# Loading v two tokens to a partition, with half-size attention tiles, wider q and k runs and a new opening order, in a fused chunk-attention and feed-forward kernel

## The chip, the cores and the metric

The kernel runs on one core of one Trainium2 chip. The metric is the device time of one execution, in microseconds (us); each kernel is run several times and the median is quoted.

Engines have these names in the profile: PE is TensorE's matmul, PEld its weight load, DVE is VectorE, ACT is ScalarE, POOL is GpSimd, SPq is the queue on which SyncE issues DMA. A matmul instruction of the program appears as one LDWEIGHTS (PEld) and one MATMUL (PE), 2,576 of each in the profile of the kernel before; the text calls the two together a *pair*.

## The reference, cut to what matters

```
q, k, v: 8 x 8 x 576 x 64 (batch, head, token, d), float32;   4608 tokens in all
for every chunk of 64 tokens of every head:
    attn = softmax(q_c @ k_c.T / 8);   out_c = attn @ v_c        # 64x64 and 64x64
x = out, heads side by side                                      # 4608 x 512
h = x @ w_in                                                     # 512 -> 2048
g = h * sigmoid(beta * h)                                        # beta: one number per hidden unit
result = g @ w_out                                               # 2048 -> 512
```

The kernel works in nine blocks of 512 tokens (eight chunks, 8 heads). For each block it computes the attention, then the two large products. `mm1` is a group of four 128x512 matmuls of the hidden layer, `mm2` one of the output layer; a block has 16 of each.

## The kernel before

The parts that the change touches. A matmul of the attention uses one quarter of TensorE's array: a 64x64 tile. (The profile writes 64*64 for it, and 128*128 for a large matmul.) The trace of this kernel shows the score pairs in fours, one for each quarter: four start 3 to 4 ns apart, then there is a step, mostly of 21 or 22 ns, to the next four, about 32 ns from group to group. `scores` puts out 16 pairs per call (half of them in the opening), `attend` 32.

```
def load_beta():                                  # 2,048 descriptors of 4 bytes
    e.dma_start(beta_raw[:, :], beta.rearrange("(t p) -> p t", p=128))
    ...                                           # beta_half = beta_raw * 0.5 on VectorE

def load_qk(blk, which, halves=(0, 1)):           # runs of 1 KB: 4 tokens x 64 x 4 bytes
    ...
    a = src[b][:, 64 * c:64 * (c + m), :].rearrange("(hp hb) (s i) d -> s hp hb (i d)", hb=2, i=4)

def load_v(blk, pairs=(0, 1, 2, 3)):              # runs of 256 bytes: one token to a partition
    ...
    e.dma_start(vstage[r:r + 64 * m, s, at // 2, h, :],
                v[b][h, 64 * c:64 * (c + m), :].rearrange("h t d -> t h d"))

def scores(blk, hp, halves=(0, 1)):
    ...
    for cc in range(2 * halves[0], 2 * halves[-1] + 2):
        for g in range(2):
            for hb in range(2):
                def f(e, cc=cc, g=g, hb=hb):
                    r, col = slice(64 * hb, 64 * hb + 64), 256 * w + 64 * cc
                    return e.matmul(A[64 * g:64 * g + 64, 2 * u + hb, col:col + 64],
                                    kT[r, 2 * cc + g, :], qT[r, 2 * cc + g, :])
...
def attend(blk, u, ps=A, psname="A", bank0=0, halves=(0, 1)):
    ...
                return e.matmul(ps[64 * half:64 * half + 64, bank, col:col + 65],
                                E[r, 2 * u + hb, 256 * w + 64 * cc:256 * w + 64 * cc + 64],
                                v_bf[r, sa, cc, 4 * u + 2 * w + hb, 0:65])
...
first = [ (load_qk, 0, 0, (1,)), (cast_qk, 0, 0, 1, "act"), ...     # hand-made order of blocks 0 to 2
```

From block 3 on a fixed plan interleaves attention with `mm1` and `mm2`; per block there are two bursts of score matmuls and two of V products, 32 pairs each, with large matmuls between them.

The softmax here doesn't subtract the row's maximum and nothing guards it: scores larger than these inputs give would overflow.

Of the kernel before, what the change touches and what calls it, by code (L numbers as in the profile page):

```python
# [166 lines left out]
def bass_chunk_attention__then__act_swish_beta_kernel(nc, q, k, v, w_in, w_out, beta, out):  # L167
# [8 lines left out]
    with ExitStack() as es:  # L176
# [7 lines left out]
        beta_raw = sb("beta_raw", [128, NT], F32)  # L184
# [6 lines left out]
        qkstage = sb("qkstage", [128, NQS, 2, 2, 4, 256], F32)  # L191
        vstage = sb("vstage", [128, NVS, 4, H, 64], F32)
        qkcast = sb("qkcast", [128, 2, 4, 4, 2, 64], BF16)
        qkT = sb("qkT", [128, 2, 4, 4, 128], BF16)
        qkO = sb("qkO", [128, 4, 2, 4, 32, 4], BF16)
        NVA = 2
        v_bf = sb("v_bf", [128, NVA, 4, H, 66], BF16)
        E = sb("E", [128, 4, 512], BF16)
        rec = sb("rec", [128, 2, 16], F32)
        x_sb = sb("x_sb", [128, 2, 2, 4, 128], BF16)  # L200
        NXT = 2
        xT = sb("xT", [128, NXT, 2, 2, 4, 128], BF16)
# [13 lines left out]
        def chunk_pairs(blk):  # L216

            if blk == REST:
                return [(b, CPB - 1, 1, b) for b in range(B)]
            return [(blk - (blk > REST), c, 2, c) for c in range(0, 8, 2)]  # L220


        def make_constants():
            P.op("pool", lambda e: e.memset(identity[:, :], 1.0), writes=[K("identity")])
            P.op("pool", lambda e: e.affine_select(
                out=identity[:, :], in_=identity[:, :], compare_op=ALU.is_equal, fill=0.0,
                base=0, pattern=[[-1, 128]], channel_multiplier=1),
                reads=[K("identity")], writes=[K("identity")])
            for sa in range(NVA):
                P.op("pool", lambda e, sa=sa: e.memset(v_bf[:, sa, :, :, 64:66], 1.0),  # L230
                     writes=[K("ones", sa)])
# [5 lines left out]

        def load_beta():
            def f(e):
                with nc.allow_non_contiguous_dma(reason="beta is tiny"):  # L240
                    return e.dma_start(beta_raw[:, :], beta.rearrange("(t p) -> p t", p=128))
            P.dma("act", f, writes=[K("beta_raw")])
            P.op("dve", lambda e: e.tensor_single_scalar(
                beta_half[:, :], beta_raw[:, :], 0.5, ALU.mult),
                reads=[K("beta_raw")], writes=[K("beta_half")])
# [4 lines left out]
        def load_qk(blk, which, halves=(0, 1)):  # L250
            s, src = blk % NQS, (q, k)[which]
            for b, c, m, at in chunk_pairs(blk):
                if at // 4 not in halves:
                    continue

                def f(e, b=b, c=c, m=m, at=at):
                    a = src[b][:, 64 * c:64 * (c + m), :].rearrange(
                        "(hp hb) (s i) d -> s hp hb (i d)", hb=2, i=4)
                    r = 64 * (at % 2)
                    return e.dma_start(qkstage[r:r + 64 * m, s, which, :, at // 2, :], a)  # L260
                P.dma("sp", f, writes=[K("qkstage", s, which, at + i, v=blk) for i in range(m)])

        def load_v(blk, pairs=(0, 1, 2, 3)):
            s, us, h = blk % NVS, (0, 1), slice(0, H)
            for b, c, m, at in chunk_pairs(blk):
                if at // 2 not in pairs:
                    continue

                def f(e, b=b, c=c, at=at, m=m):
                    r = 64 * (at % 2)  # L270
                    return e.dma_start(vstage[r:r + 64 * m, s, at // 2, h, :],  # L271
                                       v[b][h, 64 * c:64 * (c + m), :].rearrange("h t d -> t h d"))
                P.dma("sp", f, writes=[K("vstage", s, u, at + i, v=blk)
                                       for u in us for i in range(m)])
# [43 lines left out]
        def cast_qk(blk, which, half, eng):  # L318
            s, r = blk % NQS, slice(2 * half, 2 * half + 2)
            copy_cast(eng, qkcast[:, which, r, :, :, :].rearrange("p n i h d -> p h (n i) d"),  # L320
                      qkstage[:, s, which, :, r, :].rearrange("p h n (i d) -> p h (n i) d", i=4),
                      [K("qkstage", s, which, 4 * half + c, v=blk) for c in range(4)],
# [9 lines left out]
        def order_qk(blk, hp, eng):  # L332
            copy_cast(eng, qkO[:, hp, :, :, :, :].rearrange("k w n t i -> k (w n) t i"),
                      qkT[:, :, :, :, :].rearrange("k w n i (t h) -> k h (w n) t i", h=4)[:, hp],
# [3 lines left out]
        def transpose_pe(blk, which, half, ps, psname, bank, eng):  # L338
            r = slice(2 * half, 2 * half + 2)
            dst = ps[:, bank, :].bitcast(BF16).rearrange("p (i n t) -> p i n t", n=2, i=4)  # L340
            for n in range(2):
                for i in range(4):
                    P.op("pe", lambda e, n=n, i=i: e.transpose(  # L343
                        dst[:, i, n, :],
                        qkcast[:, which, 2 * half + n, i, :, :].rearrange("p h d -> p (h d)"),
                        identity[:, :]),
                        reads=[K("qkcast", which, half, v=blk), K("identity")],
                        writes=[K(psname, bank, v=("t", blk, which, half))])
            copy_cast(eng, qkO[:, :, which, r, :, :].rearrange("k h n t i -> k h (n t) i"),
                      dst.rearrange("k i n (t h) -> k h (n t) i", h=4),  # L350
# [3 lines left out]
        def cast_v(blk, eng, cc, us=(0, 1)):  # L354
            s, sa, h = blk % NVS, blk % NVA, slice(4 * us[0], 4 * us[-1] + 4)
            copy_cast(eng, v_bf[:, sa, cc, h, 0:64], vstage[:, s, cc, h, :],
                      [K("vstage", s, u, 2 * cc + g, v=blk) for u in us for g in range(2)],
                      [K("v_bf", sa, u, cc, v=blk) for u in us])



        def scores(blk, hp, halves=(0, 1)):
            u, w = divmod(hp, 2)
            qT, kT = (qkO[:, hp, which, :, :, :].rearrange("k n (c t) i -> k (n c) (t i)", c=2)
                      for which in range(2))
            for cc in range(2 * halves[0], 2 * halves[-1] + 2):
                for g in range(2):
                    for hb in range(2):
                        def f(e, cc=cc, g=g, hb=hb):
                            r, col = slice(64 * hb, 64 * hb + 64), 256 * w + 64 * cc  # L370
                            return e.matmul(A[64 * g:64 * g + 64, 2 * u + hb, col:col + 64],  # L371
                                            kT[r, 2 * cc + g, :], qT[r, 2 * cc + g, :])
                        P.op("pe", f, reads=[K("qkO", hp, which, half, v=blk)
                                             for which in range(2) for half in halves],
                             writes=[K("A", 2 * u + hb, v=("s", blk, halves))])

        def exp(blk, bank):
            P.op("act", lambda e: e.activation(E[:, bank, :], A[:, bank, :], AF.Exp, scale=0.125),  # L378
                 reads=[K("A", bank, v=("s", blk, (0, 1)))],
                 writes=[K("E", bank, half, v=blk) for half in range(2)])  # L380

        def exp_half(blk, u, half):
            dst, src = (a[:, 2 * u:2 * u + 2, :].rearrange("p b (w c) -> p b w c", w=2)[
                :, :, :, 128 * half:128 * half + 128] for a in (E, A))
            P.op("act", lambda e: e.activation(dst, src, AF.Exp, scale=0.125),  # L385
                 reads=[K("A", 2 * u + hb, v=("s", blk, (half,))) for hb in range(2)],
                 writes=[K("E", 2 * u + hb, half, v=blk) for hb in range(2)])
# [3 lines left out]


        def attend(blk, u, ps=A, psname="A", bank0=0, halves=(0, 1)):
            sa, nh = blk % NVA, len(halves)
            for cc in range(2 * halves[0], 2 * halves[-1] + 2):
                for hb in range(2):
                    for w in range(2):
                        for g in range(2):
                            def f(e, cc=cc, hb=hb, w=w, g=g):
                                r, half = slice(64 * g, 64 * g + 64), g ^ w  # L400
                                bank = bank0 + nh * g + cc // 2 - halves[0]
                                col = 65 * (2 * (cc % 2) + hb)
                                return e.matmul(  # L403
# [105 lines left out]
        def attention(blk, t0, u):  # L509
            for hp in range(4):  # L510
                at(t0 + (hp // 2) * u, scores, blk, hp)
# [216 lines left out]
```

## Time and profile before

| | before |
|---|---|
| time, median of 3 runs (range) | 301.92 us (301.12 to 302.09) |
| span of the profiled execution | 299.5 us |
| first `mm1` matmul starts | 21.54 us |
| first score burst of block 4 | 110.28 us |
| first score burst of block 8 | 228.73 us |
| last matmul starts | 295.97 us |
| block period in the steady part | 29.56 us |

First, a few lines of the profile page: busy time by engine, DMA packets, the queue that brings instructions, and the group of score matmuls (line, engine, operation, tile and shape, count, then busy us and mean ns).

```profile
PE 281.0 (94%) x2576; PEld 145.5 (49%) x2576; DVE 149.3 (50%) x244; ACT 158.7 (53%) x268; POOL 104.5 (35%) x95
...
DMA packets 106627, 55.98 MB, mean 187 GB/s; under 512 B 78952, under 2 KB 98408, under 8 KB 106600
...
q8 instruction: 20, 0.33, 0.5%
...
L371 PE MATMUL A<-qkO 64*64 64x64 bf16 x576 | 9.0, 200 | 1.1 <-ACT E L385 1.1
```

PE is busy 94% of the span, so the time can fall only by less work on PE or by fewer waits of PE.

Next, the chain of waits in a regular block (start, length, what), then the timeline of PE around one score burst.

```profile
169.47 0.37 PE A L371 x32
169.84 0.97 PE F L464 x4
...
199.02 0.38 PE A L371 x32
199.40 0.75 PE F L464 x3
```

```profile
168.44 1.03 PE L482 MATMUL F<-w_out_bf,g 128*128 128x512 bf16 x4
169.40 0.44 PE L371 MATMUL A<-qkO 64*64 64x64 bf16 x32
169.77 1.04 PE L464 MATMUL F<-xT,w_in_bf 128*128 128x512 bf16 x4
```

The chain returns to the same point after 199.40 - 169.84 = 29.56 us, and holds nothing but PE: a steady block is TensorE's own time. By the single records a burst takes 309 ns from the last large matmul to its first start, 253 ns between its first and last start, and 125 ns to the next large matmul. Of these 687 ns, 216 are the large matmul's own, so a burst costs 0.471 us.

The opening, in the timeline of PE and of the other engines (waits stand in brackets):

```profile
6.19 5.61 SPq L271 DMA_DIRECT2D vstage<-in_v_dram  x4
...
16.87 0.17 DVE L243 TENSOR_SCALAR beta_half<-beta_raw 128x16 f32<-128x16 f32 x1 [2.43 <-DMA beta_raw<-in_moe_beta_dram]
...
16.96 0.62 POOL L316 CAST v_bf<-vstage 128x512 bf16<-128x512 f32 x1 [1.51 <-DMA vstage<-in_v_dram]
```

```profile
17.63 0.44 PE L403 MATMUL F<-v_bf,E 64*64 64x65 bf16 x16 [1.06 <-POOL v_bf L316]
...
19.14 1.03 PE L444 MATMUL F<-identity,x_sb 128*128 128x128 bf16 x8 [0.86 <-DVE x_sb L426]
...
21.54 1.01 PE L464 MATMUL F<-xT,w_in_bf 128*128 128x256 bf16 x4
```

SyncE spends 5.61 us issuing four loads of v; the last v tile and beta both hold the work up to about 17 us. That is what the change is aimed at.

### The profile page before, as it was taken

How to read it: one execution, taken by the hardware profiler on the slowest of the kernel's cores; microseconds unless marked ns; L12 is line 12 of the kernel's file. 1: busy time of each engine (PE TensorE's matmuls, PEld its weight loads, DVE VectorE, ACT ScalarE, POOL GpSimd, SP SyncE). 2: the span in 40 equal slices, each digit the busy share in tenths (PEclk: the TensorE clock that was granted, in tenths of full speed). 3: DMA queues.
4: the chain of work that ended last, by engine and by line, in shares of the span. 5: the costliest groups of instructions: out<-in, count | busy, mean ns of one | idle time of the engine just before them, and what ended most of it. 6: DMA issues, size and time to landing. Idle time of an engine off the chain costs nothing.

```text
span 299.5 us, 6088 instructions
## 1 busy us (share of the span) xinstructions
PE 281.0 (94%) x2576; PEld 145.5 (49%) x2576; DVE 149.3 (50%) x244; ACT 158.7 (53%) x268; POOL 104.5 (35%) x95
## 2 busy tenths in 40 slices
PE   0669999999999999999999999999999999999995
PEld 0447855766554444444444444444444444444442
DVE  0458876766698533643364337433733373443300
ACT  3558964675676546444644464446444745544311
POOL 1135653634062594069177409540750000000000
PEclk9999999999999999999999999999999999999999
DMA  6999999999999968999947992898471122000121
GB/s 176 237 334 376 338 246 348 302 326 252 212 283 179 230 192 229 178 271 314 184 113 232 267 207 70 245 277 157 65 91 39 45 70 72 36 35 35 63 79 70
DMA packets 106627, 55.98 MB, mean 187 GB/s; under 512 B 78952, under 2 KB 98408, under 8 KB 106600
## 3 DMA queue, kind: packets, MB, share of 16 engines
q1 hardware_dynamic: 99408, 46.15, 64.9%
q10 hardware_dynamic: 7192, 9.45, 9.2%
q8 instruction: 20, 0.33, 0.5%
q14 instruction: 7, 0.06, 0.1%
HBM read 36.71 MB, written 9.44 MB: 154 GB/s over the span
## 4 chain that ended last, share of the span: by engine, by line
PE 79%; SPq 9%; DMA 8%; POOL 1%; ACT 1%; DVE 1%; issue 1%; ACTq 0%
PE F L482 39%; PE F L464 34%; SPq L260 5%; DMA wstage<-in_moe_w_out_dram 3%; DMA qkstage<-in_q_dram 2%; PE A L464 2%; DMA vstage<-in_v_dram 2%; SPq L289 2%; PE A L403 2%; SPq L271 2%; PE A L371 2%; POOL w_out_bf L305 1%; DVE qkO L316 0%; ACTq L496 0%; ACT ostage L488 0%
## 5 line engine op out<-in xcount | busy, mean ns | idle before, releaser
L482 PE MATMUL F<-w_out_bf,g 128*128 128x512 bf16 x576 | 145.0, 379 | 0.8 <-POOL w_out_bf L305 0.8
L473 DVE SCALAR_TENSOR_TENSOR g<-tt,F 128x512 bf16<-128x512 bf16 (+1 forms) x140 | 88.5, 634 | 108.1 <-ACT tt L469 107.8
L469 ACT ACTIVATE tt<-F,beta_half 128x512 bf16<-128x512 f32 (+1 forms) x140 | 89.9, 645 | 96.4 <-PE F L464 92.8
L464 PE MATMUL F<-xT,w_in_bf 128*128 128x512 bf16 (+1 forms) x560 | 130.3, 359 | 0.2
L482 PEld LDWEIGHTS F<-w_out_bf,g 128*128 128x128 bf16 x576 | 55.2, 98 | 63.3 <-POOL w_out_bf L305 0.9
L464 PEld LDWEIGHTS F<-xT,w_in_bf 128*128 128x128 bf16 x560 | 53.0, 98 | 52.2 <-DVE g L473 0.5
L316 POOL COPY qkO<-qkT 128x1024 bf16<-128x1024 bf16 x21 | 41.6, 2026 | 56.5 <-DMA qkT<-qkcast 47.3
L316 POOL CAST qkcast<-qkstage 128x1024 bf16<-128x1024 f32 x29 | 30.8, 1073 | 35.2 <-DMA qkstage<-in_k_dram 20.1
L488 ACT ACTIVATE ostage<-F 128x512 f32<-128x512 f32 x36 | 21.5, 598 | 19.7 <-PE F L482 19.7
L426 DVE TENSOR_TENSOR x_sb<-A,rec 128x1024 bf16<-128x1024 f32 (+1 forms) x19 | 20.6, 1084 | 0.7
L464 PE MATMUL A<-xT,w_in_bf 128*128 128x256 bf16 x144 | 19.9, 275 | 0.9 <-POOL w_in_bf L295 0.9
L469 ACT ACTIVATE tt<-A,beta_half 128x256 bf16<-128x256 f32 x36 | 16.4, 474 | 6.3 <-PE A L464 6.3
L316 POOL CAST v_bf<-vstage 128x512 bf16<-128x512 f32 x28 | 16.5, 625 | 6.5 <-DMA vstage<-in_v_dram 6.5
L473 DVE SCALAR_TENSOR_TENSOR g<-tt,A 128x256 bf16<-128x256 bf16 x36 | 14.7, 418 | 4.9 <-ACT tt L469 4.6
L378 ACT ACTIVATE E<-A 128x512 bf16<-128x512 f32 x28 | 16.3, 592 | 0.7 <-PE A L371 0.7
L464 PEld LDWEIGHTS A<-xT,w_in_bf 128*128 128x128 bf16 x144 | 13.9, 99 | 4.4 <-DVE g L473 1.5
L343 PE MATMUL A<-identity,qkcast 128*128 128x128 bf16 x48 | 4.5, 249 | 7.9 <-ACT qkcast L314 7.4
L305 POOL CAST w_out_bf<-wstage 128x2048 bf16<-128x2048 f32 x4 | 7.6, 1896 | 11.0 <-DMA wstage<-in_moe_w_out_dram 11.0
L371 PEld LDWEIGHTS A<-qkO 64*64 64x64 bf16 x576 | 6.6, 113 | 8.1 <-issue 4.4
L295 POOL CAST w_in_bf<-wstage 128x2048 bf16<-128x2048 f32 (+1 forms) x5 | 7.8, 1555 | 7.2 <-DMA wstage<-in_moe_w_in_dram 5.9
L371 PE MATMUL A<-qkO 64*64 64x64 bf16 x576 | 9.0, 200 | 1.1 <-ACT E L385 1.1
L403 PEld LDWEIGHTS A<-v_bf,E 64*64 64x64 bf16 x528 | 6.0, 109 | 7.0 <-issue 4.7
(36 smaller groups left out, 81.0 us busy)
## 6 DMA issues: line engine op xcount, KB each, us to landing
out_dram<-ostage ACTq DMA_DIRECT2D x36, 256.0 KB, 2.9
qkstage<-in_q_dram SPq DMA_DIRECT2D x32, 256.0 KB, 4.8
qkstage<-in_k_dram SPq DMA_DIRECT2D x32, 256.0 KB, 5.9
vstage<-in_v_dram SPq DMA_DIRECT2D x32, 256.0 KB, 6.6
wstage<-in_moe_w_out_dram SPq DMA_DIRECT2D x4, 1024.0 KB, 9.4
wstage<-in_moe_w_in_dram SPq DMA_DIRECT2D x3, 1024.0 KB, 11.9
wstage<-in_moe_w_in_dram SPq DMA_DIRECT2D x2, 512.0 KB, 9.3
qkstage<-in_q_dram SPq DMA_DIRECT2D x8, 128.0 KB, 3.7
```

Of the source, the lines that this page charges most:

```text
L260: return e.dma_start(qkstage[r:r + 64 * m, s, which, :, at // 2, :], a)
L305: P.op("pool", lambda e: e.tensor_copy(w_out_bf[:, 4 * j:4 * j + 4, :], wstage[:, j, :].rearrange("p (t d) -> p t d", t=4)), reads=[K("wst ...
L316: P.op(eng, lambda e: e.tensor_copy(dst, src), reads, writes)
L371: return e.matmul(A[64 * g:64 * g + 64, 2 * u + hb, col:col + 64], kT[r, 2 * cc + g, :], qT[r, 2 * cc + g, :])
L378: P.op("act", lambda e: e.activation(E[:, bank, :], A[:, bank, :], AF.Exp, scale=0.125), reads=[K("A", bank, v=("s", blk, (0, 1)))], write ...
L403: return e.matmul(ps[64 * half:64 * half + 64, bank, col:col + 65], E[r, 2 * u + hb, 256 * w + 64 * cc:256 * w + 64 * cc + 64], v_bf[r, sa ...
L426: P.op("dve", lambda e: e.tensor_tensor(dst, o[:, :, :, 0:64], r.unsqueeze(3).to_broadcast([128, nb, 4, 64]), ALU.mult), reads=src + [K("r ...
L464: P.op("pe", lambda e, c=c: e.matmul(ps[:, bank, r], w_in_bf[:, c, 128 * t:128 * t + 128], x_of(sx, c, halves), start=(c == 0), stop=(c == ...
L469: P.op("act", lambda e: e.activation(tt[:, T % NTT, r], ps[:, bank, r], AF.Tanh, scale=beta_half[:, t:t + 1]), reads=[K(psname, bank, v=(" ...
L473: P.op("dve", lambda e: e.scalar_tensor_tensor(g2[:, sg, t, r], tt[:, T % NTT, r], 1.0, ps[:, bank, r], ALU.add, ALU.mult), reads=[K(psnam ...
L482: P.op("pe", lambda e, t=t: e.matmul(ps[:, bank, :], g2[:, sg, t, 128 * s:128 * s + 128], w_out_bf[:, t, :], start=(t == 0), stop=(t == NT ...
L488: P.op("act", lambda e: e.activation(ostage[:, N % NOS, :], ps[:, bank, :], AF.Copy, scale=0.5), reads=[K(psname, bank, v=("o", N))], writ ...
```

## The change

The intent: v in runs of 512 bytes and q and k in runs of 2 KB (fewer, larger packets and half the issues), beta in 64 descriptors instead of 2,048, and an opening order remade for the earlier data. With two tokens of v on a partition, a chunk of 64 tokens lies on 32 partitions. So the score matmul of a chunk becomes two of 64 rows by 32 columns (even and odd keys), and its V product two of 32 rows by 64 columns that add up in PSUM. These are half the size and twice the number, so that eight instead of four cover the array.

```
-        beta_raw = sb("beta_raw", [128, NT], F32)
+        beta_raw = sb("beta_raw", [128, 32], F32)
+        beta_T = sb("beta_T", [128, 32], F32)
...                                            # load_beta
-                    return e.dma_start(beta_raw[:, :], beta.rearrange("(t p) -> p t", p=128))
+            for j in range(4):
+                P.dma("act", lambda e, j=j: e.dma_start(
+                    beta_raw[32 * j:32 * j + NT, :],
+                    beta.rearrange("(t j p) -> j t p", j=4, p=32)[j]), ...)
+        def turn_beta():                       # a 32x32 transpose on VectorE, then the half
...                                            # load_qk
-                        "(hp hb) (s i) d -> s hp hb (i d)", hb=2, i=4)
+                        "(hp hb) (s i) d -> s hp hb (i d)", hb=2, i=8)
...                                            # load_v
-                                       v[b][h, 64 * c:64 * (c + m), :].rearrange("h t d -> t h d"))
+                        a = v[b][h, 64 * c:64 * (c + m), :].rearrange("h (p i) d -> p h (i d)", i=2)
...                                            # scores
-                            return e.matmul(A[64 * g:64 * g + 64, 2 * u + hb, col:col + 64],
-                                            kT[r, 2 * cc + g, :], qT[r, 2 * cc + g, :])
+            for i in range(2):
+                for c in range(4):
+                    for hb in range(2):
+                            return e.matmul(A[32 * c:32 * c + 32, 2 * half + hb, col:col + 64],
+                                            kT[r, c, i::2], qT[r, c, :])
...                                            # attend
+                                        E[r, 2 * half + hb, at:at + 64],
+                                        v_bf[r, sa, half, 2 * hp + hb, i, 0:65],
+                                        start=(i == 0), stop=(i == 1))
...                                            # and the order of blocks 0 to 2, wholly new;
                                               # from block 3 on the same places in the plan
```

## The prediction

> **What bounds the kernel now.** TensorE, after a slow opening. The table of busy time by stretches shows it busy nearly all the time from 50 us, clock 1.00. A token block takes 29.56 us (same point of successive blocks in the chain of waits: 169.84, 199.40): 32 groups of four 128x512 matmuls at 0.864 us = 27.65, plus 1.91 for attention (four bursts of 32 matmuls, 0.48 us each, about 0.09 of it the mode change). Such spacings, summed over all matmuls, give 274 us of work in the 299.5 us span: 17 us are lost before the first hidden-layer matmul at 21.5 us, 5 between 21.5 and 80, 3.4 in the tail.
>
> **What the opening waits for** (timeline of 0 to 36 us): loads. First q lands at 4.9 us, last q/k about 11.0, last v tile about 16.9. SyncE spends 0.65 us per q/k issue and 1.4 per v issue, 11 us for block 0. In the DMA records a 256 B packet took 23 ns, 1 KB 53, 2 KB 93; the 4 B beta packets 10 ns each, 2048 of them 1.3 us over 16 engines.
>
> **What changes.**
> - DMA, block 0: q/k 6.8 us to 5.9; v 5.9 to about 4 (estimate: 512 B near 32 ns); beta 1.3 to 0. Some 4 us less before block 0 is complete, 2.8 us less per later block. SyncE issues: about 6 us instead of 11 (estimate).
> - TensorE: score and V-product matmuls double, 1152 to 2304. [...] In the trace four tiles start 3.3 ns apart and the next four follow after 32 ns, so eight starts (27 ns) should just fit into the same 32. [...] I expect 0.48 to 0.55 us per burst of 64: 0 to 2.5 us in all.
> - Exp, normalize, casts, transposes keep their sizes.
> - New order, estimated from measured durations: q/k complete near 9 us, scores of half 0 near 10.5, last V product 15.7, four normalizations on DVE (0.9 each) to 17.4, turns and copies to 18. First hidden-layer matmul at 18.0 us (17 to 19.5) instead of 21.5. w_in comes 4 us earlier, so most of this survives; stalls between there and 80 us go from 5 to 3 to 5.
>
> **Sum:** 301.9 - 3.5 (opening) - 1.3 (later stalls) + 1.0 (tiles) - 0.5 (beta, order) = 297.6 us. Range 293.8 to 301.3. Faster by over 2% (under 295.9): 0.26; within 2%: 0.68; slower: 0.06.
>
> **What would show it.** First hidden-layer matmul near 18 us; last v cast near 14; block period 29.6 to 29.9; DMA packets under 512 B down from 79k to a few thousand; TensorE gaps between 20 and 80 us no larger than before.
>
> **What would make it wrong.**
> - TensorE cannot be fed more than 32 load-and-multiply pairs in a row at 4 ns a pair: this trace has no longer burst. [...]
> - Four row tiles writing four PSUM banks, or stride-2 stationary reads, run slower.
> - The order lets the hidden layer begin even earlier (16.5), or DMA relief removes nearly all later stalls: over 2% faster.
> - ACT or DVE, 0.43 to 0.47 us per half tile against 0.44 of TensorE, become the limit once loads do not.

The term for the tiles, +1.0, stands on the trace's 3.3 ns and 32 ns alone: that eight half-size tiles would start as close together as four old ones, and so 0.48 to 0.55 us a burst, was the author's estimate. What the text calls the mode change is the passage from large to small matmuls: 309 ns from start to start there instead of 216, hence its 0.09 us.

## The result

The changed kernel takes **312.61 us** (310.55 to 313.4, four runs, correct) against 301.88 us (301.12 to 302.09) of the kernel before on the same chip. The ratio is 1.035, with a 95% interval of 1.030 to 1.040: slower. A ratio here is the mean time of one kernel's fast runs over the mean of the other's fast runs of the same rounds, so it isn't quite the ratio of the medians.

| start of | before, us | after, us | difference |
|---|---|---|---|
| first `mm1` matmul | 21.54 | 22.83 | +1.29 |
| first score burst of block 4 | 110.28 | 116.95 | +6.67 |
| first score burst of block 8 | 228.73 | 239.83 | +11.10 |
| last matmul | 295.97 | 308.06 | +12.09 |

So three losses have to be explained: an opening that should have been 3.5 us shorter and isn't, about 5.4 us between the opening and block 4, and 4.43 us over four regular blocks, which is 1.11 us a block.

The page of the changed kernel, the same lines:

```profile
PE 287.9 (92%) x3687; PEld 155.4 (50%) x3728; DVE 147.5 (47%) x250; ACT 159.2 (51%) x269; POOL 102.1 (33%) x92
...
DMA packets 76220, 56.12 MB, mean 180 GB/s; under 512 B 39320, under 2 KB 58776, under 8 KB 76184
...
q8 instruction: 29, 0.48, 0.6%
...
L376 PE MATMUL A<-qkO 64*32 64x64 bf16 x1152 | 13.0, 199 | 1.8 <-DVE qkO L322 1.1
```

The number of pairs has grown from 2,576 to 3,728 (by PEld), and the packets of instructions with it, from 20 to 29. The packets under 512 B have halved, to 39,320.

The chain of waits in a regular block, and the timeline around one score burst:

```profile
178.29 0.65 PE A L376 x64
178.94 0.97 PE F L452 x4
...
208.92 0.65 PE A L376 x64
209.57 0.97 PE F L452 x4
```

```profile
177.26 1.03 PE L470 MATMUL F<-w_out_bf,g 128*128 128x512 bf16 x4
178.22 0.72 PE L376 MATMUL A<-qkO 64*32 64x64 bf16 x64
178.87 1.04 PE L452 MATMUL F<-xT,w_in_bf 128*128 128x512 bf16 x4
```

The period is now 209.57 - 178.94 = 30.63 us, 1.07 more, and again the chain holds almost only PE. The records of the burst's 64 matmul starts have this form: the first 32 follow each other in 3 to 5 ns (one step of 16), then comes a single gap of 105 ns, and then the rest follow at 8 or 9 ns each (two steps of 34). A burst spans 537 ns for scores and 523 for V products, with 309 ns before and 118 after it. By the same reckoning it costs 0.748 us (309 + 537 + 118 - 216) or 0.734 us instead of 0.471. Two bursts of each kind a block give 2 x 0.277 + 2 x 0.263 = 1.08 us, which is the lengthening of the period.

The opening, on the DMA side first: SyncE's issue of v takes 4.70 us from 3.58 instead of 5.61 from 6.19, and the last v cast starts at 15.17 us, 1.8 us earlier. PE's timeline then shows what came of it:

```profile
3.58 4.70 SPq L278 DMA_DIRECT2D vstage<-in_v_dram  x4
...
15.17 0.42 DVE L322 CAST v_bf<-vstage 128x512 bf16<-128x512 f32 x1
```

```profile
15.31 0.44 PE L399 MATMUL F<-v_bf,E 32*64 32x65 bf16 x30
18.99 0.26 PE L399 MATMUL F<-v_bf,E 32*64 32x65 bf16 x2 [3.24 <-issue]
18.99 0.56 PE L399 MATMUL A<-v_bf,E 32*64 32x65 bf16 x32
...
22.83 1.49 PE L452 MATMUL A<-xT,w_in_bf 128*128 128x256 bf16 x6
```

```profile
42.38 0.51 PE L399 MATMUL A<-v_bf,E 32*64 32x65 bf16 x11
45.67 0.29 PE L399 MATMUL A<-v_bf,E 32*64 32x65 bf16 x21 [2.77 <-issue]
```

PE stops twice in the middle of a burst: at 15.5 us after 30 of 32 pairs, all of whose data had the same producers, and at 42.7 us after 11 of 32. "issue" means that the profile shows nothing that PE waited for, neither a tile nor a semaphore. (From start to start, counting weight loads too, these gaps are 3.48 and 2.97 us.) After the second one the clock drops, as the table by stretches shows (stretch, length, busy us of PE, PEld, DVE, ACT, POOL, then granted clock, DMA share and GB/s):

```profile
45.70:46.20 0.50, 0.50 (x24) 0.43 (x25) 0.04 (x1) 0.00 (x0) 0.03 (x1) 1.00 1.04 385
46.20:49.60 3.40, 3.18 (x44) 1.60 (x44) 1.91 (x5) 0.78 (x2) 2.52 (x2) 0.50 1.09 357
49.60:53.00 3.40, 3.35 (x84) 2.08 (x84) 2.09 (x6) 1.37 (x3) 0.89 (x2) 0.99 1.12 328
```

TensorE runs at half clock for 3.4 us. That is about 1.7 us of lost work (an estimate: half of 3.4). The drop comes at 46.22 us, 0.56 us after the end of the gap of 2.97 us. That the gap is its cause isn't shown: in run 5 below a gap of 1.87 us was, in the profiled execution of run 3 one of 2.14 us was not. The fastest of the four runs, 310.55 us, was the only one with a mean granted clock of 1.000; the other three had 0.995 and took 312.5 to 313.4 us.

The opening runs at half clock too, in both kernels, which the "1.00" of the tables hides: the trace's first clock record stands at 22.9 us (before) and 25.7 us (after). Until then `mm1` matmuls of 256 columns start 213 ns apart, afterwards 109. Eight such matmuls of the changed kernel on either side of that point (timeline of PE from 22.8 to 27 us):

```profile
22.83 1.91 PE L452 MATMUL A<-xT,w_in_bf 128*128 128x256 bf16 x8
...
26.00 1.04 PE L452 MATMUL F<-xT,w_in_bf 128*128 128x256 bf16 x8
```

So the changed kernel works on `mm1` for 2.9 us at half clock, the kernel before for 1.4; that is some 0.8 us more of lost work (an estimate: half of the difference). It also means that the start of the first `mm1` alone does not measure a lead: what comes before that point goes at half speed (213 ns instead of 109 for those matmuls).

### Where the gaps come from: the position in the program

If one counts PE's and PEld's instructions from the beginning (with the few waits of PE's own sequencer that the trace has, 5 before the first gap and 11 before the second), the gap at 15.5 us comes after the 449th and the one at 42.7 us after the 1,216th. With 64 added these are 513 and 1,280: a multiple of 256, or one past it. The 64 are fitted; what they stand for isn't shown (instructions that stand ahead of the profiled ones would give such a constant). Beside that the DMA records show one 16 KB packet on the instruction queue for about every 256 instructions: 20 packets for 5,152 in the kernel before, 29 for 7,456 in the changed one, with two instructions to each pair. The first column below is the boundary, in program order counted with those 64.

| kernel, boundary | PE reached the 256 before it at | packet ran | PE stopped | PE went on | after the packet's end |
|---|---|---|---|---|---|
| before, 512 | 15.54 us | 18.83 to 19.99 | no (reached it at 26.57) | | |
| after, 512 | 12.07 us | 16.61 to 17.72 | 15.51 | 18.98 | 1.26 us |
| after, 1280 | 38.92 us | 43.07 to 44.23 | 42.70 | 45.66 | 1.43 us |
| after, 2048 | 64.56 us | 65.73 to 66.71 | 67.23 | 68.12 | 1.42 us |

These read as one story: each packet is the next 256 instructions, and at all three stops TensorE went on only after the packet had ended, 1.26 to 1.43 us later. In the busy opening the first packet begins 3.3 us (before) and 4.5 us (after) after PE reached the 256 before it. In the kernel before, these 256 instructions last 11.0 us (15.54 to 26.57), and nothing stops. In the changed kernel bursts use them up in 3.4 us (12.07 to 15.51). (These times are counted from PE's own place. Packets can also come ahead of it: late in the changed kernel's trace, five of the last seven packets begin 0.4 to 2.0 us before PE reaches that place. So they are not the delay of a request.) In all, the changed kernel loses 7.4 us in such gaps; the kernel before, none.

So far this is a reading of one trace. The runs below test it.

### The profile page after: what moved, and what is told of

Read it like the earlier page. It is cut to its first block, busy times and chain, and to the rows that moved or that the text cites. A ratio compares the mean times of both kernels' runs of the same rounds, so it can differ in the third digit from the quotient of the medians.

```text
span 311.6 us, 8295 instructions
## 1 busy us (share of the span) xinstructions
PE 287.9 (92%) x3687; PEld 155.4 (50%) x3728; DVE 147.5 (47%) x250; ACT 159.2 (51%) x269; POOL 102.1 (33%) x92
## 2 busy tenths in 40 slices
DMA packets 76220, 56.12 MB, mean 180 GB/s; under 512 B 39320, under 2 KB 58776, under 8 KB 76184
## 4 chain that ended last, share of the span: by engine, by line
PE 84%; DVE 6%; issue 4%; DMA 3%; ACT 1%; ACTq 1%; DVEq 0%
PE F L470 38%; PE F L452 35%; DVE g L461 4%; PE A L399 3%; PE A L376 3%; PE A L452 3%; DMA beta_raw<-in_moe_beta_dram 2%; DMA qkstage<-in_q_dram 1%; DVE qkO L322 1%; PE A L433 1%; DVE x_sb L417 1%; ACT tt L457 1%; PE F L433 1%; PE A L347 0%; ACTq L484 0%
## 5 line engine op out<-in xcount | busy, mean ns | idle before, releaser
L457 ACT ACTIVATE tt<-F,beta_half 128x512 bf16<-128x512 f32 (+1 forms) x149 | 93.9, 635 | 104.0 <-PE F L452 100.4
L470 PE MATMUL F<-w_out_bf,g 128*128 128x512 bf16 x535 | 138.3, 381 | 3.3 <-issue 1.5
L452 PE MATMUL F<-xT,w_in_bf 128*128 128x512 bf16 (+1 forms) x596 | 135.4, 354 | 0.2 <-DVE g L461 0.2
L322 POOL CAST qkcast<-qkstage 128x1024 bf16<-128x1024 f32 x27 | 27.9, 1045 | 30.5 <-DMA qkstage<-in_q_dram 15.2
L384 ACT ACTIVATE E<-A 128x512 bf16<-128x512 f32 x36 | 20.6, 592 | 2.8 <-PE A L376 2.8
L452 PE MATMUL A<-xT,w_in_bf 128*128 128x256 bf16 x108 | 16.0, 286 | 0.0
L399 PEld LDWEIGHTS A<-v_bf,E 32*64 32x64 bf16 x1056 | 9.8, 105 | 11.0 <-issue 8.0
L399 PE MATMUL A<-v_bf,E 32*64 32x65 bf16 x1056 | 12.4, 204 | 2.8 <-issue 2.8
L376 PE MATMUL A<-qkO 64*32 64x64 bf16 x1152 | 13.0, 199 | 1.8 <-DVE qkO L322 1.1
L457 ACT ACTIVATE tt<-A,beta_half 128x256 bf16<-128x256 f32 x27 | 12.5, 477 | 4.2 <-PE A L452 2.9
L376 PEld LDWEIGHTS A<-qkO 64*32 64x32 bf16 x1152 | 10.7, 91 | 7.9 <-issue 5.5
```

What stands on the lines that cost most here:

```text
L322: P.op(eng, lambda e: e.tensor_copy(dst, src), reads, writes)
L376: return e.matmul(A[32 * c:32 * c + 32, 2 * half + hb, col:col + 64], kT[r, c, i::2], qT[r, c, :])
L384: P.op("act", lambda e: e.activation(E[:, bank, :], A[:, bank, :], AF.Exp, scale=0.125), reads=[K("A", bank, v=("s", blk))], writes=[K("E" ...
L399: return e.matmul(ps[64 * w:64 * w + 64, c, col:col + 65], E[r, 2 * half + hb, at:at + 64], v_bf[r, sa, half, 2 * hp + hb, i, 0:65], start ...
L452: P.op("pe", lambda e, c=c: e.matmul(ps[:, bank, r], w_in_bf[:, c, 128 * t:128 * t + 128], x_of(sx, c, halves), start=(c == 0), stop=(c == ...
L457: P.op("act", lambda e: e.activation(tt[:, T % NTT, r], ps[:, bank, r], AF.Tanh, scale=beta_half[:, t:t + 1]), reads=[K(psname, bank, v=(" ...
```

## The experiments

The theory, called F, is *feeding*: TensorE loses time because more instructions have to be brought to it, on two scales. In a burst, the pairs after the first 32 come slower (8 to 9 ns each after a gap of 105 ns, instead of 3 to 5 ns); and in the opening program packets land too late for bursts (the gaps of 3.48 and 2.97 us). The rivals are T, that half-size *tiles* are slow as such (four row tiles that write four PSUM banks, strided weights), and O, that the new opening *order* waits more by itself.

### 1. The changed kernel with v by one token again

The change but for its first part: v and tiles as before (1,152 attention matmuls, bursts of 32), with the q, k and beta loads and the opening order of the changed kernel. One thing comes with it: in this order v of blocks 0 and 1 is loaded in twice as many issues as in either kernel (8 a block instead of 4; block 0 holds SyncE 7.84 us instead of 4.70).

```
-  a = v[b][h, ...].rearrange("h (p i) d -> p h (i d)", i=2);  vstage [128, NVS, 2, H, 128]
+  a = v[b][h, ...].rearrange("h t d -> t h d");               vstage [128, NVS, 2, 2, H, 64]
-  e.matmul(A[32 * c:32 * c + 32, 2 * half + hb, col:col + 64], kT[r, c, i::2], qT[r, c, :])
+  e.matmul(A[64 * g:64 * g + 64, 2 * half + hb, col:col + 64], kT[r, 2 * cc + g, :], qT[r, 2 * cc + g, :])
```

> The changed kernel with one part undone: v again by one token a partition (256 B runs), so scores and V products again in four 64x64 tiles and 1152 matmuls; order, q/k in 2 KB, beta in 64 descriptors kept. Theory F (feed: beyond 32 load-and-multiply pairs TensorE is fed a pair in 8.3 ns after a pause of 105 ns, and 256-instruction refills of its program come too late when it runs through instructions too fast): block period back from 30.63 to 29.56 us, no gap of about 3 us before the first hidden-layer matmul, which comes at 19 to 20 us instead of 22.8; total 295 to 299 us. Rival O (the new order of the opening is itself worse): period back too, but first hidden-layer matmul still after 22 us, total about 302 to 304.

Measured: 302.37 us (301.51 to 303.69), ratio to the kernel before 1.004, interval 1.000 to 1.008. Nearly all of the loss is gone, but the total that F expected, 295 to 299 us, was missed. The steady period is back at 29.56 us and the first `mm1` comes at 19.28 us. Of the gaps at program boundaries one is left, 0.95 us at 65.7 us: it comes after 1,473 instructions (counted by weight loads; with 64: 1,537, one past a multiple of 256), and PE goes on 1.59 us after the end of the packet. (In blocks 1 to 3 the scores still stand 64 pairs in a row, by the new order.) This is the timeline of PE at the first `mm1`, and two later waits:

```profile
18.62 0.63 PE L435 MATMUL A<-identity,x_sb 128*128 128x128 bf16 x4
19.28 1.44 PE L454 MATMUL A<-xT,w_in_bf 128*128 128x256 bf16 x6
...
45.50 0.32 PE L404 MATMUL A<-v_bf,E 64*64 64x65 bf16 x16 [1.27 <-DVE v_bf L327]
...
66.66 1.38 PE L454 MATMUL F<-xT,w_in_bf 128*128 128x256 bf16 x11 [0.68 <-issue]
```

What follows: O falls as the cause of the loss against the kernel before, because the same order with the old tiles opens 2.26 us earlier than it. But this kernel gains nothing either: its first score burst of block 4 starts at 110.51 us, against 110.28. The lead is gone by then. More than half of it goes to the half clock, which lasts until 23.3 us here: at 25.6 us 41 `mm1` matmuls have started against 32 in the kernel before, which is 1.0 us (9 x 0.109, an estimate). The rest goes in waits: the first wait above is for a cast of v of block 1, the second a refill. So the prediction's "most of this survives" did not hold here even without the half tiles. Run 7 has the same q, k and beta loads in the old order, and it is faster by 1.4% (ratio 0.990, interval 0.987 to 0.993). Whether the new order or the doubled issues of v cost this one that gain, no run separates.

### 2. The kernel before with every attention matmul of blocks 3 to 8 issued as two

Same data, same 64x64 tiles, same order; only each matmul is cut into two of half the moving columns. That doubles the instructions and leaves out everything else of the change.

```
+  cuts = (0, 32, 64) if blk > 2 else (0, 64)
+  for x, y in zip(cuts, cuts[1:]):
       return e.matmul(A[64*g:64*g + 64, 2*u + hb, col + x:col + y], kT[r, 2*cc + g, :], qT[r, 2*cc + g, x:y])
```

> The kernel before with nothing changed but that from block 3 on each score and V-product matmul is issued as two of half the columns (32+32, 33+32), same data, same four 64x64 tiles. Theory F: bursts of 64 pairs span about 500 to 540 ns instead of 253, block period 30.5 to 30.7 us instead of 29.56, six blocks give +6 us: 307 to 309 us. Rival T (eight half-size tiles are slower in the array: four row tiles to four PSUM banks, stride-2 stationary reads): tiles are unchanged and each matmul half as long, so bursts stay under 350 ns, period under 29.9, total under 304 us.

Measured: 308.72 us (308.54 to 309.25), ratio 1.025, interval 1.022 to 1.027. The same timeline of PE:

```profile
172.08 1.03 PE L487 MATMUL F<-w_out_bf,g 128*128 128x512 bf16 x4
173.04 0.73 PE L373 MATMUL A<-qkO 64*64 64x32 bf16 x64
173.70 0.61 PE L469 MATMUL F<-xT,w_in_bf 128*128 128x512 bf16 x2
```

A burst of 64 score pairs on old tiles takes as long in this view (0.73) as one on half-size tiles (0.72), and the period is 30.84 us (203.88 - 173.04), a little over the 30.5 to 30.7 expected; bursts span 550 ns (scores) and 628 (V products), not 500 to 540. What follows: twice the matmuls, each half as long, lengthen the regular blocks without any half-size tile. But the single records show another form than in the changed kernel: no gap of 105 ns, and the first 32 score pairs of a burst (263 ns) are hardly faster than the last 32 (276 ns). Four old tiles take about 32 ns for each group of four pairs in the kernel before as well, with 64 columns there and 32 here. So this run agrees with F in its total, and doesn't show what slows eight tiles after 32 pairs; runs 5 and 6 do.

### 3. The same in blocks 0 to 2 only

```
+  cuts = (0, 32, 64) if blk <= 2 else (0, 64)
```

> The kernel before with the same doubling in blocks 0 to 2 alone. Theory F: the opening reaches the refills of TensorE's program earlier than they land: at least one gap of 1 to 3.5 us put down to issue before 50 us, next to a 16 KB transfer of the instruction queue, and 64-pair bursts in blocks 1 and 2; total 304 to 309 us. Rivals T and O: no more than +1 us, under 303 us.

Measured: 308.94 us (308.43 to 309.31), ratio 1.025, interval 1.023 to 1.028. Later blocks have the old period. The gap of the changed kernel appears in the kernel before, again in the middle of a burst:

```profile
17.47 0.62 PE L408 MATMUL A<-v_bf,E 64*64 64x33 bf16 x30
21.90 0.23 PE L408 MATMUL A<-v_bf,E 64*64 64x33 bf16 x1 [3.81 <-issue]
```

It lies after the same 449 instructions as in the changed kernel, although the orders differ. Two more, at 45.5 and 51.3 us, lie after 1,216 and 1,471 records (with 64: 1,280 and 1,535; before the last one, one or two matmul records are missing, 728 against 730 weight loads). PE goes on 1.46, 1.26 and 1.42 us after the end of the packet. In all 7.65 us are lost in such gaps, and the kernel is 7 us slower. What follows: more instructions in the opening are enough to make the gaps.

### 4. The changed kernel with 192 small weight loads put first on PE

If the gap belongs to a position in the program, it moves when instructions are put ahead of it; if it belongs to a certain tile or wait, it doesn't. The loads read a constant and nothing uses them.

```
+  for _ in range(192): e.ldweights(identity[:, 0:16])          # ahead of everything else on PE
```

> The changed kernel with 192 weight loads of 16 columns (results unused) ahead of everything on TensorE, in time it spends waiting for the first q; nothing else. They shift the page boundaries of TensorE's program by 192 instructions. If the 3.2 us gap at 15.7 us is TensorE out of program (third page of 256 instructions [...] there at 19 us): [...] no gap where it was (in the V products after the second scores); a new gap opens where the shifted boundary is reached, about 66 instructions later, near 16.5 us, of 2 to 4 us, so the time stays within 2 us of the changed kernel. If the gap is a wait for data or a hold-up of the array: it stays at the same instruction.

When a packet is asked for isn't shown, only when it ran. That the old gap goes was the author's estimate; what the text calls a page is the 256 instructions of one packet.

Measured: 310.57 us (309.56 to 312.0), ratio 1.029. The first gap had been after pair 222; it moved to after pair 254 and one weight load more, 65 loads and matmuls further. Counted as above it moved from 449 to 705, which is 256 exactly, 192 of them added ones; 705 + 64 = 769 is one past the next multiple of 256.

```profile
16.66 0.44 PE L403 MATMUL A<-v_bf,E 32*64 32x65 bf16 x30 [0.75 <-ACT E L388]
21.80 0.26 PE L403 MATMUL A<-v_bf,E 32*64 32x65 bf16 x2 [4.70 <-issue]
```

The position was predicted almost to the instruction ("about 66"). The size was not: 4.70 us against 2 to 4 expected, because the packet began 5.7 us after PE had reached the 256 before it (13.81 to 19.48), and ran until 20.52. PE went on 1.28 us after that. Two smaller gaps, 1.14 and 1.00 us, stand at the boundaries 1,536 and 1,792. What follows: the gaps are program refills. Why packets begin so late, 0.4 to 8.8 us after PE reached that place in the first 70 us of the three kernels before, changed and padded, stays open; the DMA engines were nearly always busy then (90% or more in each slice of the page from 7.5 us on in the kernel before, from 7.8 to 62 us in the changed one), which may be the reason, and no run varied that alone.

### 5. The changed kernel with bursts cut to 32 pairs from block 3 on

Between each 32 pairs stand four large matmuls.

```
+  # while issuing the plan: when a burst would pass 32 pairs, take the next large group first
+  if run + n > 32: pop the next mm1 or mm2 and issue it; run = 0
```

> The changed kernel, from block 3 on with a group of four hidden or output matmuls between every 32 small ones, so that no burst is over 32 pairs; same instructions. Theory F: no pause of 105 ns and no 8.3 ns spacing any more, each half burst 0.35 to 0.37 us with its mode change, against 0.74 for the whole, so period 30.5 to 30.6 us instead of 30.63 and 0 to 1 us less in all: the mode changes eat what the feed gives back. If the feed were the only cost and mode changes free: period 29.8 us, 5 us less.

Measured: 311.75 us (311.42 to 312.2), ratio 1.0345, interval 1.031 to 1.038. The chain of waits:

```profile
177.15 0.24 PE A L376 x32
177.39 0.97 PE F L452 x4
178.36 0.24 PE A L376 x32
178.60 0.16 issue
```

A burst of 32 half-size pairs now spans 122 ns (scores) or 144 ns, so the rate of 3 to 4 ns holds through it, and the slow second half is gone. But each such burst again pays 309 ns before it and about 122 ns after it: by the same reckoning 0.34 to 0.36 us, so 0.67 to 0.72 for 64 pairs in two bursts, against 0.73 to 0.75 in one. The three refill gaps of the opening are still there, 3.15, 1.87 and 0.89 us. What follows: what slows the second half of a burst is that 32 pairs have gone before it without a break, since the same pairs run fast after a break; short bursts cure that and give it back as more passages from large to small matmuls and back (309 ns instead of 216 between starts on the way in, about 122 on the way out). Why it is 32 pairs, and what goes on in the 309 ns, no run shows.

### 6. The changed kernel with one token of each pair (wrong result), twice

Half of the pairs are left out; loads, casts, order and half-size tiles stay. The result is wrong. What is left is about what the change would be worth if half-size tiles needed no more instructions than before.

```
-            for i in range(2):          # in scores and in attend
+            for i in range(1):          # and exp reads the same columns twice
```

> WRONG RESULT ON PURPOSE. The changed kernel with only the first token of each pair multiplied (half of the score and V-product matmuls, the eight half-size tiles, order, loads and packets all kept; exp reads the same columns twice). Theory F: bursts of 32 pairs span 140 to 220 ns, block period 29.1 to 29.6 us, no gap put down to issue over 1 us before 50 us, first hidden-layer matmul near 19 us, total 294 to 299 us. Rival T (small tiles slow as such): half of the excess remains, period 30.0 or more, total over 303 us.

Measured, first time: 294.68, 296.24 and 296.2 us, ratio 0.981, interval 0.977 to 0.985. A fourth run took 582.49 us, 1.97 times the median of the other three, at a recorded clock of 1.000, and it was the profiled one; it is left out. So the kernel was run once more for its profile.

> Wrong result on purpose, the same kernel as the earlier half-token run, whose one profiled execution fell in a disturbed state: the changed kernel with one token of each pair multiplied, so eight half tiles in bursts of 32 pairs. If the cost of the tiles lies in going beyond 32 pairs without a pause: block period 29.0 to 29.5 us (at or below before's 29.56, since eight tiles start 3 to 4 ns apart and save the 32 ns step of four tiles), no TensorE gap over 2 us at the instruction counts 449 and 1216 of the changed kernel, first hidden-layer matmul 18 to 19.3 us. If eight half tiles are slow as such: period above 30 us although the pairs are half as many.

Measured, second time: 293.89 us (one run, so its state is unknown), first `mm1` at 19.11 us, no gap at a program boundary, and a period of 192.55 - 163.50 = 29.05 us between score bursts. The timeline:

```profile
162.76 0.81 PE L472 MATMUL F<-w_out_bf,g 128*128 128x512 bf16 x3
163.50 0.31 PE L376 MATMUL A<-qkO 64*32 64x64 bf16 x32
163.74 1.04 PE L454 MATMUL F<-xT,w_in_bf 128*128 128x512 bf16 x4
```

A burst of 32 half-size pairs is faster (0.31) than one of 32 old ones (0.44). What follows: T falls. Half-size tiles aren't slow: with eight of them 32 score pairs start within 120 ns, 3.9 ns from pair to pair, with four old tiles in the kernel before within 253 ns, 8.2 ns. In this second run all that F expected held. This run also shows what the second half of the pairs costs, their own array time included: 16 to 19 us lie between its runs and the median of the changed kernel (exponentials and casts have the same sizes in both).

### 7. The loads alone, on the kernel before

If instructions are the loss, then the parts of the change that add none should gain. First q, k and beta together, with old v, tiles and order, beta placed in the middle of the opening:

```
-  "(hp hb) (s i) d -> s hp hb (i d)", hb=2, i=4        +  ..., i=8
-  beta: one load of 2,048 descriptors                  +  four loads, 64 descriptors, then a transpose
```

> The kernel before, own order, v and tiles, with q and k in 2 KB runs and beta in 64 descriptors alone. If packets are what the opening waits for: 2 us less DMA before block 0 is complete, first hidden-layer matmul at 20 to 21 us instead of 21.5, total 299 to 301 us. If the order has to change with it: within 0.5 us of before.

Measured: 301.28 us (300.94 to 302.82), ratio 1.001. This missed because of my placing of beta: the four issues held ScalarE's queue for 2.54 us, between two exponentials, and beta came so late that VectorE waited 7.74 us, until 21.19. The first `mm1` started at 25.62 us, and yet the time was equal. So a start that is 4 us later was made good: the 65th weight load of the output layer starts at 72.55 us, at 72.31 in the kernel before. The start of `mm1` isn't all that counts.

The same with beta issued first of all, and turned just before the hidden layer:

> The kernel before with q and k in 2 KB runs, and beta in 64 descriptors issued first on the ScalarE queue and turned only just before the hidden layer (in the earlier run of this kind beta was issued in the middle of the opening, where four issues held ScalarE's exp back by 3 us and VectorE waited 7.7 us for the landing). If that misplacement was all: first hidden-layer matmul at 20 to 21.5 us, total 299 to 300.5 us, 0.3 to 1 per cent faster than before. If loads of blocks 1 and 2 set the time at 60 us whatever the start: within 0.5 us of before.

Measured: **298.22 us** (297.73 to 299.55, six runs) against 301.19; ratio 0.990, interval 0.987 to 0.993. The first `mm1` starts at 20.13 us, the first score burst of block 4 at 106.78 (before 110.28), and the last matmul at 292.47 (before 295.97): a lead of 3.5 us. It isn't the lead of the opening that survives: the pairs stand in the same order as in the kernel before, and pair by pair this one leads by 1.40 us at the first `mm1`, trails by 0.28 at pair 200 (about 25 us), since its half clock lasts until 25.0 us, and leads by 3.50 from pair 750 on (66 us). What it gains it gains after 25 us: from there to 110 us PE waits 0.3 us, in the kernel before 2.7. The version with beta in the middle gains as much after the opening, from 4.11 us behind to 0.24. This version is correct and beats both kernels.

Then each of the two alone, both runs beside the same runs of the kernel before:

> The kernel before with q and k alone in 2 KB runs (beta still 2,048 descriptors at its old place, v, tiles and order as before). If the q/k runs carry the gain of the run with q/k and beta together (298.2 us, first hidden-layer matmul at 20.13 us): first hidden-layer matmul at 20.1 to 20.7 us and 298.0 to 299.5 us. If the beta load carries it: first hidden-layer matmul at 21.2 to 21.6 us and 301 to 302 us.

Measured: 300.19 us (299.05 to 302.05), ratio 0.997, interval 0.993 to 1.000; first `mm1` at 20.49 us.

> The kernel before with beta alone in 64 descriptors, issued first on ScalarE's queue (q, k, v, tiles and order as before). If the q/k runs carry the gain: 301 to 302 us, first hidden-layer matmul within 0.5 us of 21.5. If the beta load carries it: 298 to 299.5 us, first hidden-layer matmul near 20.1.

Measured: 300.3 us (299.52 to 300.76), ratio 0.996, interval 0.993 to 0.999; first `mm1` at 20.77 us.

Neither expectation fits: each carries about a third of the gain (0.3 and 0.4%), and the two together have about 1%. The intervals are too wide to say that the sum is really more than its parts. Here too a program refill shows, small: q and k alone stop PE for 0.76 us at 65.5 us, beta alone for 0.24 us at 67.3, both together not at all. Whether it matters for the sum was not tested.

## Why the prediction was wrong

The prediction was 297.6 us, with a range to 301.3 and a chance of 0.06 for slower by over 2%. It was 312.61.

- **The step that failed first is the term "tiles (+1.0)", "0.48 to 0.55 us per burst of 64".** Measured: 0.734 and 0.748 us, some 0.27 more a burst; over nine blocks of four bursts about 9.6 us (9 x 1.07, an estimate from the regular blocks). The start rate that it was costed with was right: eight half-size tiles start 3 to 4 ns apart, and eight in 32 ns had been assumed. But that rate holds for 32 pairs in a row only, as runs 5 and 6 show (122 and 120 ns for 32 score pairs, 537 for 64). That more than 32 pairs in a row could be slower stood in the prediction's own list of what would make it wrong. The size that it gave was half of what was measured. In the measured burst the later pairs come at 8 to 9 ns, and one gap of about 105 ns lies before them.
- **A step was missing: program refills.** Nothing in the prediction asks how instructions reach TensorE. Gaps of 3.48, 2.97 and 0.90 us, and 3.4 us at half clock after one of them, are the price in the first 70 us. The first gap ended "first hidden-layer matmul at 18.0 us": the V products that should have ended at 15.7 stood still from 15.5 to 19.0, and it started at 22.83. With fewer instructions and the same order it started at 19.28 (old tiles) and 19.11 (half the pairs), so 18.0 was also too early by about 1.2 us.
- **"Most of this survives" was wrong.** The old tiles in the new order led by 2.26 us at the first `mm1` and by nothing at block 4. Where q, k and beta alone were changed, the lead of 1.41 us was gone at 25 us, and one of 3.50 us came afterwards from fewer waits. The prediction took a microsecond of earlier start for a microsecond; TensorE runs at half clock until 22.6 to 28.0 us in these traces (the first clock record of each), and beyond that the next blocks' data have to come earlier too.
- **The DMA terms were mostly right, and a little large.** SyncE's issues for block 0 took 7.5 us (0.81 to 8.31) instead of the 6 estimated, and of 11 before. The last v cast started at 15.17 us; expected near 14. Packets under 512 B fell to 39,320, not to "a few thousand": 36,864 of those left are 256 B packets of the DMA transposes (12 of x with 1,024 each, 6 of q and k with 4,096), which I had not subtracted. "Beta 1.3 to 0" forgot latency: in the changed kernel VectorE takes beta only at 12.86 us, and this is a wait in its opening chain (6.08 us of DMA).
- **"TensorE gaps between 20 and 80 us no larger than before"** was the right thing to look at: the largest was 2.97 us, 0.98 in the kernel before.

How the losses add up is settled in kind, less so in amounts. Bursts (9.6 us), refills (7.4) and the half clock after the second gap (1.7) together are 18.7 us, with the longer half clock of the opening (0.8) 19.5; the span grew by 12.1, and the changed kernel with half its pairs gained 7.4 on the span of the kernel before (299.5 to 292.1). So the parts must overlap; a refill that falls where TensorE would have waited for a load anyway may be how, but no run shows it. It stays open, too, why bursts in the last 90 us of the changed kernel span 485 to 498 ns instead of 523 to 537.

## What to carry to other kernels

Count instructions as well as array time: a split that halves a small matmul and keeps the array as full was not free here once a burst was longer than the 32 pairs that start fast in a row (0.27 us more a burst of 64), and in a start that consisted of bursts the program's own packets, one for about 256 instructions, came too late and left TensorE standing for 3.48 and 2.97 us, while the DMA engines were busy all the time (the profile gives them a share of 1.06 and 1.05 in these two stretches). When an engine stops inside a burst for no shown reason, count its instructions from the beginning and look for a fixed step (256 here); padding it with harmless instructions shows whether the gap belongs to a position in the program (192 weight loads moved it here from after the 449th instruction to after the 705th). Don't judge an opening by the start of its first large matmul alone; compare the same instruction, later. And split a bundle of changes before judging it: here the small parts alone, q and k runs and beta, gave 1% while the bundle cost over 3%.
